# Weight loads of a second MoE issued by GpSimd instead of SyncE, and its raw tiles loaded a group earlier

## The chip, the cores and the metric

The kernel runs on one core of a Trainium2 chip. The metric is the device time of one execution in microseconds (us). TensorE (PE) multiplies matrices; VectorE (DVE), ScalarE (ACT) and GpSimd (POOL) work on tiles; SyncE (SP) and POOL issue the DMA transfers (loads and stores), which run on 16 DMA engines.

## The reference

Talking-heads attention, then two feed-forward blocks ("MoE" by name) on the 1792 tokens that come out of it:

```python
scores = scale * q @ k^T            # (4, 12, 448, 448)
attn = softmax(einsum(scores, w_pre)); attn = einsum(attn, w_post)
x = (attn @ v) as 1792 x 768
h = x @ w_in;  x = layernorm(h * softmax(h)) * g_ln @ w_out    # d_ff 1024
h = x @ w2_in; out = max(h, 0)**2 @ w2_out                     # d_ff 2048
```

All is float32; two of the four weight matrices come as float64 words, w2_in and w2_out among them, and the kernel makes float32 of them itself.

## The kernel before, in words

Every product is made of three float32r products: each operand is split into a rounded part (ACT's copy) and the rest (a subtraction on POOL or DVE). The kernel has three stages: the attention (to about 400 us), the first MoE (to about 655 us) and the second MoE (the rest). The change lies in the second MoE, apart from the place of some constants.

**The second MoE** goes over the tokens in two passes of 896, and in each over d_ff in 8 groups of 256 columns (`NE = 8`). `q` counts the groups of both passes, 0 to 15. In group q, PE makes the hidden products of the group (`prod`, line 1107: in the first pass four plain ones, "22", "21", "12", "11"; in the second pass seven, of sums and differences of the quadrants) and, in between, the output products of the group before, seven tiles y of 128 tokens (`y2`, line 1178; `ps_y` has two buffers). A list sets the order of a group's slots; in the first pass it is `SEQ_P = ["22", 4, "21", 5, 6, 3, "12", 0, 1, 2, "11"]`, where the numbers are y tiles. Tiles y of group 0 are copied out of PSUM by ACT (line 1187), those of the later groups are added by DVE (line 1189). ACT makes the squared relu of each hidden product (lines 1123 to 1125), DVE its rest (line 1120).

In each slot `k` further work is set by `plan(q)`: `split_ti` (line 1035 on ACT, line 1036 on POOL) makes `ti` from `ra`, the raw tile of w2_in; `split_to` (line 1043 on ACT, line 1044 on POOL) makes `to` from `ro`, the raw tile of w2_out. Each raw tile has one buffer, so the next load of it, `load_ra` (line 985) and `load_ro` (line 996), stands right behind the splits that read it:

```python
at(7, split_to, q, 0)
at(8, split_to, q, 1)
at(8, load_ro, n)
at(10, split_ti, n, "a11")
at(10, split_ti, n, "a12")
at(10, load_ra, n + 1)
```

**The stream.** `w2stream` makes float32 of the 96 pieces (128 x 256) of w2_in and w2_out; 60 of them during the first MoE, the rest in q = 0 to 5 of the second. A piece has a load of float64 words to `nraw` (four buffers; line 793, SP), a square on ACT (line 803) and a multiplication on POOL (line 804), which make a mask `nt`, three steps on DVE (lines 828, 832, 834) and a store to DRAM (line 811, SP), from where `ra` and `ro` are loaded later. `steps2(n)` advances the stream by n of its steps, three a piece.

**The second pass's tokens.** `mix_second` loads x2D tiles `xb` (line 917, SP), makes their differences on DVE (line 925) and stores these to `xtD` (line 931); it advances once a slot in q = 6. In q = 7 and 8 `load_xc` (line 966, SP) loads the operands `xr`, and `split_xc` splits them on ACT (line 977) and DVE (line 978) into `xc`. The buffers of `xb` are those in which the stream's `nt` lay.

Each engine works through its own instructions in the order in which the program names them, and a DMA issue that has to wait holds up everything behind it in its engine's queue.

Of the kernel before, what the change touches and what calls it, by code (L numbers as in the profile page):

```python
# [7 lines left out]
F32 = mybir.dt.float32  # L8
# [10 lines left out]
def kernel(  # L19
# [16 lines left out]
    nc = tc.nc  # L36
    B, D, _ = qT.shape
    H = w_pre.shape[0]
    S = v.shape[1]
    NT, DM = out.shape  # L40
    F1 = w1_in.shape[1]
# [7 lines left out]
    RH = R // 2  # L49
# [4 lines left out]

    ctx.enter_context(tc.manual_schedule())
    const = ctx.enter_context(tc.tile_pool(name="const", bufs=1, side="left"))
    mixc = tc.tile_pool(name="mixc", bufs=1, side="right")
    mixc_p = mixc.__enter__()
    dram = ctx.enter_context(tc.tile_pool(name="dram", bufs=1, space=bass.MemoryType.DRAM))
    xD = dram.tile([DM, NT], F32, name="xD")  # L60
    x2D = dram.tile([DM, NT], F32, name="x2D")
# [3 lines left out]
    w2oD = dram.tile([F2, DM], F32, name="w2oD")  # L65
    HT = NT // 4
    xtD = [dram.tile([4 * (DM // 2), HT], F32, name=f"xtD{i}") for i in range(2)]

    mask_sb = mixc_p.tile([128, 2, RH], F32, name="mask_sb")
    wp_raw = mixc_p.tile([128, H], F32, name="wp_raw")  # L70
    wq_raw = mixc_p.tile([128, H], F32, name="wq_raw")
    wpre_bd = mixc_p.tile([128, 64], F32, name="wpre_bd")
    wpost_bd = mixc_p.tile([128, H, RH], F32, name="wpost_bd")
    eps_sb = const.tile([128, 3], F32, name="eps_sb")
    g_sb = mixc_p.tile([128, F1 // 128], F32, name="g_sb")

    def narrow(raw, sq, t, eng=nc.vector):

# [390 lines left out]
    def run(part):  # L469
        for _ in part:  # L470
            pass
# [98 lines left out]
    for s in range(lo_s, NP + 2):  # L570
# [47 lines left out]
        for i in sorted(w1f):  # L618
            sq, t = w1f.pop(i)
# [43 lines left out]
    psa.__exit__(None, None, None)  # L663
    sspools[1].__exit__(None, None, None)
    late.__exit__(None, None, None)
    mixc.__exit__(None, None, None)


    K1 = F1 // 128
# [106 lines left out]
    NE = F2 // FE  # L776
# [76 lines left out]
    def steps2(n):  # L853
        for _ in range(n):
            next(stream, None)
# [77 lines left out]
    def mix_second():  # L933

        parts = [load_xb(1, 0), load_xb(1, 1)]
        yield True
        for c in range(HC):
            b11, b12, b21, b22 = qs = parts[c]
            for i in range(4):
                mix_x(qs, i, nc.vector)  # L940
                if i % 2:
                    yield True
            for name, b in zip(XT, (b11, b22, b12, b21)):
                store_xt(1, c, name, b)
            if c + 2 < HC:
                parts.append(load_xb(1, c + 2))
            yield True
# [3 lines left out]
    def load_xc(p, name):  # L951
        t0 = 2 * p * HT
        rs = []
        for c in range(HC):
            if ORDER.index(name) % 2:
                r = wi2a_p.tile([128, HT], F32, tag=("xb00", "xb01", "xb11")[c], name="xr", bufs=2)
            else:
                r = wi2a_p.tile([128, HT], F32, tag="xr", name="xr", bufs=3)
            if name in ("p1", "p2", "p3"):
                k, t = {"p1": (0, 0), "p2": (1, 0), "p3": (1, 1)}[name]  # L960
                r0 = (k * HC + c) * 128
                src = x2D[r0:r0 + 128, t0 + t * HT:t0 + (t + 1) * HT]
            else:
                r0 = (XT.index(name) * HC + c) * 128
                src = xtD[p][r0:r0 + 128]
            nc.sync.dma_start(out=r, in_=src)
            rs.append(r)
        xraw[p, name] = rs
# [11 lines left out]
    def load_ra(q):  # L980
        if q < NQ:
            f0 = (q % NE) * FE
            for k in range(2):
                t = wi2a_p.tile([128, HC, FE], F32, tag=f"ra{k}", name="ra", bufs=1)
                nc.sync.dma_start(
                    out=t,
                    in_=w2iD[k * HC * 128:(k + 1) * HC * 128, f0:f0 + FE].rearrange("(c p) f -> p c f", p=128),
                )
                ra[q, k] = t

    def load_ro(q):
        if q < NQ:
            for f in range(KE):
                t = m2_p.tile([128, DM], F32, tag=f"ro{f}", name="ro", bufs=1)
                r0 = (q % NE) * FE + f * 128
                nc.sync.dma_start(out=t, in_=w2oD[r0:r0 + 128, :])
                ro[q, f] = t

    def quad(q, f, k):
# [97 lines left out]
    def prod(q, name):  # L1097
        b = BANK[name]
        first = name not in ("p3", "p2", "p4")
        if first:  # L1100
            bank[b] = ps2_p.tile([128, 512], F32, tag=f"b{b}", name="ps_h2", bufs=1)
        pairs = PLAIN.get(name, ((name, name),))
        for j, (tn, xn) in enumerate(pairs):
            t = ti[q, tn]
            for c in range(HC):
                for i, (w, a) in enumerate(((0, 0), (0, 1), (1, 0))):
                    nc.tensor.matmul(  # L1107
                        out=bank[b][:, 0:HT],
                        lhsT=t[:, w, c],
                        rhs=xc[xn][:, a, c],  # L1110
                        start=(first and j == 0 and c == 0 and i == 0),
                        stop=(j == len(pairs) - 1 and c == HC - 1 and i == 2),
                        skip_group_check=not first,
                    )

    def lows():
        while low:
            r, f, t = low.pop(0)
            hi, lo = [gt[:, a, f, t * HT:(t + 1) * HT] for a in range(2)]
            nc.vector.tensor_tensor(out=lo, in0=r, in1=hi.bitcast(F32), op=ALU.subtract)  # L1120
# [75 lines left out]
    YO = [4, 5, 6, 3, 0, 1, 2]  # L1196
# [7 lines left out]
    def plan(q):  # L1204

        n = q + 1
        work = {}

        def at(k, f, *a):
            work.setdefault(k, []).append((f, a))  # L1210

        if q < SW:
            at(5, fin, q, "22")
            at(6, fin, q, "12")
            at(9, fin, q, "21")
            at(10, fin, q, "11")
# [3 lines that stand above are left out]
            if n < SW:  # L1220
                at(4, split_ti, n, "a21")
                at(4, split_ti, n, "a22")
                at(10, split_ti, n, "a11")
                at(10, split_ti, n, "a12")
            else:
                at(2, mix_w, n, 0)
                at(2, split_ti, n, "p1")
                at(3, mix_w, n, 1)
                at(3, split_ti, n, "p6")
                at(4, split_ti, n, "p5")  # L1230
                at(5, split_ti, n, "p7")
                at(10, split_ti, n, "p3")
                at(10, split_ti, n, "p2")
                at(10, split_ti, n, "p4")
            at(10, load_ra, n + 1)
        else:
            at(3, split_ti, n, "p1")
            at(3, mix_w, n, 0)
            at(4, mix_w, n, 1)
            at(5, split_ti, n, "p6")  # L1240
            at(6, split_ti, n, "p5")
            at(7, lambda q: square(hs.pop(q), 1, 1), q)
            at(7, split_ti, n, "p7")
            at(8, split_to, q, 0)
            at(10, split_ti, n, "p3")
            at(11, split_to, q, 1)
            at(11, load_ro, n)
            at(12, split_ti, n, "p2")
            at(13, split_ti, n, "p4")
            at(13, load_ra, n + 1)  # L1250
        return work

    load_ro(0)
    mx = mix_second()

# [8 lines left out]
    for q in range(NQ):  # L1264
        p = q // NE
        work = plan(q)
        if q == NE - 1:
            parts = [((1, name), c) for name in ORDER for c in range(HC)]
            load_xc(*parts[0][0])
            load_xc(*parts[HC][0])  # L1270
        seq = SEQ_P if q < SW else SEQ
        for k, x in enumerate(seq):
            if isinstance(x, str):
                prod(q, x)
                after(q, x)
            elif q:
                y2(q - 1, x)
            lows()
            for f, a in work.pop(k, []):
                f(*a)  # L1280
            if parts:
                t, c = parts[0]
                if q == NE - 1 and (t[1] in ("p2", "p4") or t[1] in ("p7", "p3") and k < 7):
                    t = None
                if t:
                    parts.pop(0)
                    split_xc(*t, c)
                    i = ORDER.index(t[1]) + 2
                    if c == HC - 1 and i < len(ORDER):
                        load_xc(1, ORDER[i])  # L1290
            if q <= NE - 3:
                if q or k > 5:
                    steps2(1 if x in YO[-3:] else 2)
            elif q == NE - 2:
                if k == 0:
                    run(stream)
                next(mx, None)
        assert not work
        if q < NE:
            assert len(narrowed) >= min(12 * (q + 2) + 6, len(w2pieces)), (q, len(narrowed))  # L1300
# [63 lines left out]
```

## Time and profile before

| | |
|---|---|
| time, median of 3 runs | 1124.88 us (1124.42 to 1127.59) |
| the profiled execution's own time | 1126.69 us |
| its span, first to last instruction | 1124.9 us |
| PE busy over the span | 1055.5 us (94%) |
| DVE, ACT, POOL busy | 680.0, 561.0, 629.8 us |
| mean granted clock of PE | 0.982 of full speed |

How to read it: the share of PE over the whole span hides that its gaps lie in places. Such places show in the windows (busy time of each engine in a stretch) and in the timeline (instructions in order of time, with the idle time before one and what ended it in square brackets).

### The profile page before, as it was taken

The numbers are of one execution on the slowest core, as the hardware profiler recorded it, in microseconds if no ns is written. First come the engines' busy times: TensorE is split into PE (matmuls) and PEld (weight loads), VectorE is DVE, ScalarE is ACT, GpSimd is POOL, SyncE is SP. The second block draws the span as 40 slices with busy tenths as digits, with TensorE's granted clock in tenths as the row PEclk, the third lists the DMA queues.
The fourth block names the chain that finished last, engine by engine and source line by source line (L and its number), as shares of the span: only waits on it lengthen the run. The fifth ranks groups of instructions, "written<-read, shape, count | busy, mean of one in ns | idle before, by whom it ended". The sixth has DMA issues, their size and how long they took to land.

```text
span 1124.9 us, 30957 instructions
## 1 busy us (share of the span) xinstructions
PE 1055.5 (94%) x12560; PEld 898.9 (80%) x12560; DVE 680.0 (60%) x1213; ACT 561.0 (50%) x1171; POOL 629.8 (56%) x808
## 2 busy tenths in 40 slices
PE   8789888988999899999999998999989999999998
PEld 3466555655666677989899998999988999999998
DVE  2556776766776625788887523677775752444444
ACT  3566566665777626533433444444324556444432
POOL 2656887877684736665564235545534565555520
PEclk8999999998999999999999999999999999999999
DMA  6686878778776634565654634444465441111102
GB/s 167 189 210 205 249 206 251 209 227 221 222 212 206 184 98 119 167 192 165 205 160 150 229 118 145 134 138 150 146 219 193 158 155 57 57 57 57 57 29 98
DMA packets 127182, 180.33 MB, mean 160 GB/s; under 512 B 24224, under 2 KB 99616, under 8 KB 127040
## 3 DMA queue, kind: packets, MB, share of 16 engines
q1 hardware_dynamic: 118196, 153.83, 45.1%
q0 software_dynamic: 6464, 22.60, 7.3%
q10 hardware_dynamic: 2380, 1.93, 0.6%
q8 instruction: 99, 1.62, 0.6%
q14 instruction: 43, 0.35, 0.1%
HBM read 101.63 MB, written 38.14 MB: 124 GB/s over the span
## 4 chain that ended last, share of the span: by engine, by line
PE 74%; DMA 8%; issue 7%; POOL 4%; ACT 3%; DVE 2%; SPq 1%; ACTq 0%; POOLq 0%; DVEq 0%
PE ps_y L1178 18%; PE ps_h L1107 14%; PE ps_o L764 9%; PE ps_h L459 9%; PE ps_ring L338 7%; PE ps_ring L299 7%; PE ps_pre L242 5%; PE ps_ring L208 4%; DMA sdst<-ssrc 4%; DMA ra<-w2iD 1%; ACT ssrc L215 1%; POOL ti L1036 1%; PE ps_tr L750 1%; POOL nt L804 1%; DMA v<-in_v_dram 1%
## 5 line engine op out<-in xcount | busy, mean ns | idle before, releaser
L1178 PE MATMUL ps_y<-to,gt 128*128 128x384 f32 x1332 | 244.6, 338 | 9.2 <-DVE y L1189 5.3
L1178 PEld LDWEIGHTS ps_y<-to,gt 128*128 128x128 f32 x1332 | 235.5, 190 | 12.5 <-ACT y L1187 3.9
L1107 PE MATMUL ps_h<-xc,ti 128*128 128x448 f32 x1080 | 227.3, 365 | 0.6 <-ACT h L1123 0.6
L1107 PEld LDWEIGHTS ps_h<-xc,ti 128*128 128x128 f32 x1080 | 201.9, 188 | 15.0 <-ACT h L1123 1.0
L299 PEld LDWEIGHTS ps_ring<-w,e 60*64 60x64 f32 (+1 forms) x5760 | 102.0, 137 | 66.5 <-issue 37.7
L318 DVE COPY at<-ps_ring 128x420 f32<-128x420 f32 x156 | 87.8, 610 | 111.3 <-PE ps_ring L299 111.2
L804 POOL TENSOR_SCALAR nt<-nt 128x256 f32<-128x256 f32 x96 | 111.5, 1161 | 64.3 <-ACT nt L803 55.2
L1189 DVE TENSOR_TENSOR y<-ps_y,y 128x768 f32<-128x768 f32 x97 | 92.3, 954 | 76.6 <-PE ps_y L1178 76.1
L299 PE MATMUL ps_ring<-w,e 60*64 60x60 f32 (+2 forms) x5760 | 110.2, 221 | 26.7 <-issue 17.5
L215 ACT COPY ssrc<-ps_ring 128x896 f32<-128x896 f32 x92 | 82.4, 907 | 102.8 <-PE ps_ring L208 80.8
L459 PE MATMUL ps_h<-w1i,xs 128*128 128x512 f32 x504 | 122.1, 400 | 0.6 <-POOL xs L704 0.6
L260 ACT ACTIVATE e<-ps_pre,nm 128x448 f32<-128x448 f32 x180 | 113.2, 639 | 15.4 <-DVE nm L253 13.5
L764 PE MATMUL ps_o<-zt,w1o 128*128 128x384 f32 (+1 forms) x720 | 120.4, 326 | 0.2 <-POOL w1o L690 0.2
L764 PEld LDWEIGHTS ps_o<-zt,w1o 128*128 128x128 f32 x720 | 117.0, 189 | 0.6 <-POOL w1o L690 0.6
L459 PEld LDWEIGHTS ps_h<-w1i,xs 128*128 128x128 f32 x504 | 95.1, 190 | 22.8 <-POOL xs L704 1.3
L253 DVE TENSOR_REDUCE nm<-ps_pre 128x1 f32<-128x448 f32 x180 | 103.3, 612 | 13.2 <-PE ps_pre L242 13.1
L338 PEld LDWEIGHTS ps_ring<-at,v 128*64 128x64 f32 x1536 | 80.7, 145 | 36.9 <-issue 12.9
L1036 POOL TENSOR_TENSOR ti<-ra,ti 128x384 fp32r<-128x384 f32 x56 | 59.5, 1075 | 89.9 <-ACT ti L1035 88.3
L208 PE MATMUL ps_ring<-k,q 64*64 64x448 f32 x752 | 100.6, 556 | 8.7 <-ACT ssrc L215 4.4
L1120 DVE TENSOR_TENSOR gt<-h,gt 128x448 fp32r<-128x448 f32 x64 | 48.9, 764 | 96.3 <-ACT gt L1125 91.6
L242 PE MATMUL ps_pre<-sdst,wpre_bd 64*64 64x448 f32 x720 | 99.5, 567 | 4.5 <-DMA sdst<-ssrc 2.5
L338 PE MATMUL ps_ring<-at,v 128*64 128x120 f32 (+1 forms) x1536 | 88.8, 274 | 14.3 <-issue 7.5
(105 smaller groups left out, 1388.3 us busy)
## 6 DMA issues: line engine op xcount, KB each, us to landing
sdst<-ssrc SPq DMA_DIRECT2D x166, 210.0 KB
nraw<-in_moe_w_in_dram SPq DMA_DIRECT2D x48, 256.0 KB
nraw<-in_moe_w_out_dram SPq DMA_DIRECT2D x48, 256.0 KB
ra<-w2iD SPq DMA_DIRECT2D x32, 384.0 KB
ro<-w2oD SPq DMA_DIRECT2D x32, 384.0 KB
w1raw<-in_moe_w_in_dram POOLq DMA_DIRECT2D x24, 256.0 KB, 6.4
w1raw<-in_moe_w_out_dram POOLq DMA_DIRECT2D x24, 256.0 KB, 5.9
w2iD<-nt SPq DMA_DIRECT2D x48, 128.0 KB
```

Source lines behind the costliest of these rows:

```text
L208: nc.tensor.matmul(out=ps[64 * u:64 * u + 64, e, 0:S], lhsT=qq[c][64 * e:64 * e + 64, p * n + u * half:p * n + u * half + 64], rhs=k[64 * ...
L215: (nc.vector.tensor_copy if dve else nc.scalar.copy)(ssrc[c][:, p:H:HP, :], ps[:, :, 0:S])
L242: nc.tensor.matmul(out=ps[b][64 * u:64 * u + 64, 0:S], lhsT=wpre_bd[64 * r:64 * r + m], rhs=ds[b][64 * r:64 * r + m], start=True, stop=True,)
L253: nc.vector.tensor_reduce(out=nm, in_=pres[s][b][:, 0:S], op=ALU.max, axis=AX.X, negate=True)
L260: nc.scalar.activation(out=e, in_=pres[s][b][:, 0:S], func=AF.Exp, bias=nms.pop((s, b)), scale=1.0, accum_out=sms[s][:, b:b + 1])
L299: nc.tensor.matmul(out=ps[64 * c:64 * c + 64, u, i0:i0 + ng * RH], lhsT=e[64 * u:64 * u + m, o:o + 64], rhs=w[64 * u:64 * u + m, b, g0:g0 ...
L338: nc.tensor.matmul(out=ps[64 * e:64 * e + 64, 0, q * 120:q * 120 + n], lhsT=t[:, g] if j < NJ else t[:, e, p], rhs=at[c][:, j * H + (g if ...
L459: nc.tensor.matmul(out=ps[:, u], lhsT=t[:, a, cc], rhs=w1i[cc][:, w, u * 512:(u + 1) * 512], start=(cc == 0 and a == 0 and w == 0), stop=( ...
L764: nc.tensor.matmul(out=ps[:, 0:width], lhsT=w1o[k][:, w, cc * 128:(cc + 1) * 128], rhs=zT[:, a, k, 0:width], start=(k == 0 and i == 0), st ...
L804: nc.gpsimd.tensor_scalar(out=t, in0=t, scalar1=2.0**-30, scalar2=2.0 - 2.0**-23, op0=ALU.is_ge, op1=ALU.mult)
L1107: nc.tensor.matmul(out=bank[b][:, 0:HT], lhsT=t[:, w, c], rhs=xc[xn][:, a, c], start=(first and j == 0 and c == 0 and i == 0), stop=(j == ...
L1178: nc.tensor.matmul(out=ps[:, u - u2[0], 0:DM // 2], lhsT=gt[:, a, f, o:o + 128], rhs=w[:, v, f, u * (DM // 2):(u + 1) * (DM // 2)], start= ...
```

## The change

Three edits. The constants of the attention (mask, w_pre, w_post, g_ln; 664 bytes a partition) move from a pool of their own on the right side of SBUF to the pool `const` on the left. The loads `ra` and `ro` are issued by GpSimd instead of SyncE. In the first pass of the second MoE the stream advances by two steps in every slot, where it advanced by one in the slots of y tiles 0, 1 and 2; and the first step of `mix_second`, which loads eight `xb` tiles, moves from the first slot of q = 6 to the end of the last slot of q = 5.

```diff
-    mixc = tc.tile_pool(name="mixc", bufs=1, side="right")
-    mixc_p = mixc.__enter__()
...
-    mask_sb = mixc_p.tile([128, 2, RH], F32, name="mask_sb")
+    mask_sb = const.tile([128, 2, RH], F32, name="mask_sb")
...
-    g_sb = mixc_p.tile([128, F1 // 128], F32, name="g_sb")
+    g_sb = const.tile([128, F1 // 128], F32, name="g_sb")
...
-    mixc.__exit__(None, None, None)
...
                 t = wi2a_p.tile([128, HC, FE], F32, tag=f"ra{k}", name="ra", bufs=1)
-                nc.sync.dma_start(
+                nc.gpsimd.dma_start(
...
-                nc.sync.dma_start(out=t, in_=w2oD[r0:r0 + 128, :])
+                nc.gpsimd.dma_start(out=t, in_=w2oD[r0:r0 + 128, :])
...
             if q <= NE - 3:
                 if q or k > 5:
-                    steps2(1 if x in YO[-3:] else 2)
-            elif q == NE - 2:
-                if k == 0:
+                    steps2(2)
+                if q == NE - 3 and k == len(seq) - 1:
                     run(stream)
+                    next(mx)
+            elif q == NE - 2 and k:
                 next(mx, None)
```

The order of instructions on three places. First SP at the start of the second MoE, where the loads of the stream begin; `x2D<-o` are the last stores of the first MoE. Before:

```order
L773 DMA x2D<-o_10064 128x256
L996 DMA ro<-w2oD 128x768 x2
L793 DMA nraw<-in_moe_w_in_dram 128x256 x3
L996 DMA ro<-w2oD 128x768 x2
L793 DMA nraw<-in_moe_w_in_dram 128x256
L985 DMA ra<-w2iD 128x3x256 x2
L793 DMA nraw<-in_moe_w_in_dram 128x256
L811 DMA w2iD<-nt 128x256
```

Now:

```order
L770 DMA x2D<-o_10060 128x256
L790 DMA nraw<-in_moe_w_in_dram 128x256 x5
L808 DMA w2iD<-nt 128x256
L790 DMA nraw<-in_moe_w_in_dram 128x256
L808 DMA w2iD<-nt 128x256
```

No ra or ro load stands between the raw loads of the stream any more. The second place is POOL in q = 0, from the splits of group 0's last `ti` on. Before:

```order
L804 TENSOR_SCALAR nt<-nt 128x256
L1044 TENSOR_TENSOR to<-ro,to 128x768
L804 TENSOR_SCALAR nt<-nt 128x256
L1044 TENSOR_TENSOR to<-ro,to 128x768
L804 TENSOR_SCALAR nt<-nt 128x256
L1036 TENSOR_TENSOR ti<-ra,ti 128x384 x2
L804 TENSOR_SCALAR nt<-nt 128x256 x3
```

Now:

```order
L801 TENSOR_SCALAR nt<-nt 128x256
L1041 TENSOR_TENSOR to<-ro,to 128x768
L801 TENSOR_SCALAR nt<-nt 128x256 x2
L1041 TENSOR_TENSOR to<-ro,to 128x768
L993 DMA ro<-w2oD 128x768 x2
L801 TENSOR_SCALAR nt<-nt 128x256
L1033 TENSOR_TENSOR ti<-ra,ti 128x384 x2
L982 DMA ra<-w2iD 128x3x256 x2
L801 TENSOR_SCALAR nt<-nt 128x256 x3
```

POOL has the four loads behind the splits that free their buffers, and one multiplication `nt` more ahead of the second `to`. The third place is SP from the end of the stream to q = 7. Before:

```order
L996 DMA ro<-w2oD 128x768 x2
L793 DMA nraw<-in_moe_w_out_dram 128x256
L985 DMA ra<-w2iD 128x3x256 x2
L811 DMA w2oD<-nt 128x256 x5
L917 DMA xb<-x2D 128x448 x8
L931 DMA xtD_72<-xb 128x448 x4
L917 DMA xb<-x2D 128x448 x4
L931 DMA xtD_72<-xb 128x448 x4
L996 DMA ro<-w2oD 128x768 x2
L931 DMA xtD_72<-xb 128x448 x4
L985 DMA ra<-w2iD 128x3x256 x2
L966 DMA xr<-x2D 128x448 x3
```

Now:

```order
L790 DMA nraw<-in_moe_w_out_dram 128x256
L808 DMA w2oD<-nt 128x256 x5
L914 DMA xb<-x2D 128x448 x8
L928 DMA xtD_69<-xb 128x448 x4
L914 DMA xb<-x2D 128x448 x4
L928 DMA xtD_69<-xb 128x448 x8
L963 DMA xr<-x2D 128x448 x3
```

Here too the ra and ro loads are gone from between the stream's stores, the xb tiles and the xr tiles; on SP alone the order of these is the same.

## Rows read from the trace of the kernel before

**Rows 1.** Windows of the two passes: start:end, length, then busy time.

```profile
640.00:887.00 247.00, 238.21 (x1291) 227.76 (x1290) 146.67 (x209) 105.88 (x209) 115.12 (x91) 0.99 0.47 151
887.00:1125.00 238.00, 233.43 (x1261) 225.86 (x1260) 110.07 (x143) 104.64 (x193) 112.18 (x96) 1.00 0.23 78
```

(The columns are PE, PEld, DVE, ACT and POOL, each with its count of instructions, then the granted clock of PE, the busy share of the DMA engines and GB/s.)

**Rows 2.** Timeline of PE in q = 1, and an ordinary y tile.

```profile
675.16 0.98 PE L1178 MATMUL ps_y<-to,gt 128*128 128x384 f32 x4 [0.28 <-POOL to L1044]
...
687.56 3.89 PE L1178 MATMUL ps_y<-to,gt 128*128 128x384 f32 x12 [3.61 <-ACT y L1187]
...
737.63 2.24 PE L1178 MATMUL ps_y<-to,gt 128*128 128x384 f32 x12
```

**Rows 3.** Timeline of PE in q = 6 and 7.

```profile
838.28 3.64 PE L1178 MATMUL ps_y<-to,gt 128*128 128x384 f32 x12 [3.11 <-DVE y L1189]
...
867.86 2.38 PE L1178 MATMUL ps_y<-to,gt 128*128 128x384 f32 x12 [0.95 <-DVE y L1189]
871.09 2.34 PE L1178 MATMUL ps_y<-to,gt 128*128 128x384 f32 x12 [0.85 <-DVE y L1189]
```

**Rows 4.** Windows around two gaps: PE busy, granted clock, DMA share, GB/s.

```profile
687.56:691.45 3.89, 3.89 (x13) 0.57 0.43 108
...
835.20:838.28 3.08, 0.00 (x1) 0.91 0.97 326
838.28:841.90 3.62, 3.62 (x13) 0.61 0.78 256
```

**Rows 5.** Timeline of ACT in q = 1.

```profile
685.37 0.43 ACT L803 ACTIVATE nt<-nraw 128x256 f32<-128x256 f32 x1 [5.56 <-DMA nraw<-in_moe_w_in_dram]
...
688.10 0.93 ACT L1035 CAST ti<-ra 128x384 fp32r<-128x384 f32 x2
...
691.49 0.80 ACT L1187 COPY y<-ps_y 128x768 f32<-128x768 f32 x1 [2.11 <-PE ps_y L1178]
...
695.13 0.55 ACT L1123 ACTIVATE h<-ps_h 128x448 f32<-128x448 f32 x1 [0.85 <-PE ps_h L1107]
...
697.22 0.80 ACT L1187 COPY y<-ps_y 128x768 f32<-128x768 f32 x1 [0.33 <-PE ps_y L1178]
```

**Rows 6.** Timeline of SP's queue at the end of q = 0.

```profile
677.89 1.53 SPq L985 DMA_DIRECT2D ra<-w2iD  x2
679.51 0.43 SPq L793 DMA_DIRECT2D nraw<-in_moe_w_in_dram  x1
```

**Rows 7.** Timeline of POOL at the end of q = 0.

```profile
671.80 1.13 POOL L804 TENSOR_SCALAR nt<-nt 128x256 f32<-128x256 f32 x1
673.01 2.10 POOL L1044 TENSOR_TENSOR to<-ro,to 128x768 fp32r<-128x768 f32 x1
...
676.61 2.41 POOL L1036 TENSOR_TENSOR ti<-ra,ti 128x384 fp32r<-128x384 f32 x2
```

**Rows 8.** Timeline of DVE in q = 0, 6 and 7.

```profile
670.04 1.96 DVE L832 SCALAR_TENSOR_TENSOR nt<-nraw,nt 128x256 uint32<-128x256 uint32 x1
...
672.66 0.41 DVE L834 SCALAR_TENSOR_TENSOR nt<-nraw,nt 128x256 uint32<-128x256 uint32 x1
...
833.83 0.63 DVE L925 TENSOR_TENSOR xb<-xb 128x448 f32<-128x448 f32 x1 [3.53 <-DMA xb<-x2D]
...
866.06 0.88 DVE L978 TENSOR_TENSOR xc<-xr,xc 128x448 fp32r<-128x448 f32 x1 [8.16 <-ACT xc L977]
```

**Rows 9.** Timeline of SP's queue in q = 6 and 7.

```profile
829.83 3.77 SPq L917 DMA_DIRECT2D xb<-x2D  x8
...
858.80 1.34 SPq L985 DMA_DIRECT2D ra<-w2iD  x2
860.19 1.43 SPq L966 DMA_DIRECT2D xr<-x2D  x3
```

**Rows 10.** Loads of v that POOL issues in the attention, line 186.

```profile
L186 POOL DMA_DIRECT2D v<-in_v_dram x12: 629/629/667, 38.6 to 330.1; - x12
...
DMA to landing us min/median/max: 4.9/6.7/9.8
```

(Duration of the issue in ns, least, median and most; then the time from issue to landing.)

More of the change, by code (lines that the diff above doesn't have):

```diff
@@ L67 @@
     xtD = [dram.tile([4 * (DM // 2), HT], F32, name=f"xtD{i}") for i in range(2)]
-    mask_sb = mixc_p.tile([128, 2, RH], F32, name="mask_sb")
[L70 to L73, printed above, removed]
+    mask_sb = const.tile([128, 2, RH], F32, name="mask_sb")
+    wp_raw = const.tile([128, H], F32, name="wp_raw")
+    wq_raw = const.tile([128, H], F32, name="wq_raw")
+    wpre_bd = const.tile([128, 64], F32, name="wpre_bd")
+    wpost_bd = const.tile([128, H, RH], F32, name="wpost_bd")
     eps_sb = const.tile([128, 3], F32, name="eps_sb")
-    g_sb = mixc_p.tile([128, F1 // 128], F32, name="g_sb")
+    g_sb = const.tile([128, F1 // 128], F32, name="g_sb")
     def narrow(raw, sq, t, eng=nc.vector):
```

## The prediction

> **What bounds the kernel now.** I read the windows first, to see where TensorE is not busy. From 640 to 887 us, which is the first pass of the second MoE, PE is busy 238.21 of 247.00 us; from 887 to the end 233.43 of 238.00 [rows 1]. So in this part PE sets the pace, POOL is busy under half of the time, and all that a better order of loads can give back is the 8.8 us of PE's gaps in the first pass, with what a gap costs behind it. The timeline of PE then names the gaps.
>
> In group q = 1 PE stops for 3.61 us at 684 us, released by ACT's copy of a y tile; at the start of the group it had stopped for 0.28 us [rows 2]. Around q = 6 and q = 7 it stops for 3.11, 0.95 and 0.85 us, each time released by DVE's add of a y tile [rows 3]. A gap costs more than its length: the 12 matmuls of a y tile take 2.24 us in the ordinary case [rows 2], but 3.89 and 3.64 us behind the two long gaps [rows 2, 3], where the granted clock fell to 0.57 and 0.61 of full speed [rows 4], that is mostly to the lower of its levels. Behind the two short ones they take 2.38 and 2.34 us [rows 3].
>
> So the gaps cost: at q = 1, 3.61 + (3.89 - 2.24) = 5.26 us; at q = 6, 3.11 + (3.64 - 2.24) = 4.51 us; at q = 7, 0.95 + 0.85 + 0.14 + 0.10 = 2.04 us. **Sum 11.8 us.**
>
> **What is late in each gap.** At q = 1 ACT sat 5.56 us before the square at 685.37, waiting for the load of a raw tile, with the y copies that PE waits for behind it in ACT's queue [rows 5]. That raw tile was issued by SP at 679.51 only, behind the two ra loads at 677.89 [rows 6], and the second of those waits for POOL's subtractions, which end at 676.61 + 2.41 = 679.02 [rows 7]. The raw tile's buffer had been free since DVE's last step on it, 672.66 + 0.41 = 673.07 [rows 8]. SP was blocked by a load whose turn had come too early.
>
> At q = 6 DVE waits 3.53 us for an xb tile before its first subtraction at 833.83, with the y adds behind it [rows 8]; SP issued the eight xb loads from 829.83 on [rows 9], at the tail of the rest of the stream. At q = 7 the first xc subtraction runs at 866.06 only, behind ACT's cast of a tile that SP loaded at 860.19, again right behind two ra loads at 858.80 [rows 8, 9].
>
> **The change, part by part.**
>
> *Constants.* 664 bytes a partition move from the first pool on the right to the first on the left. No instruction comes or goes, and nothing in this trace waits for them after the start. Price 0, and both bounds as well.
>
> *Loads by GpSimd.* SP loses its 64 ra and ro issues, each of which may wait for POOL. POOL's own subtraction is what they waited for, so on POOL they come at once. With SP free, the load for ACT at 685.37 is issued when its buffer is free, some 0.4 us after 673.07, which is 6 us earlier; even with the same 5.9 us from issue to use (679.51 to 685.37) it is there at 679.4, before y5's matmuls end. The gap of q = 1 goes. At q = 7 the loads no longer stand behind ra either, whose place in the queue held them until 858.80; the x tiles then go out behind the last xtD stores. That gap goes too.
>
> POOL pays for each issue. The nearest row is the v load, of the same 384 KB and issued by POOL in the attention: 0.629 us, and 6.7 us in the median to landing (4.9 to 9.8) [rows 10]. ra is in three pieces a partition where v is in one; so I take 0.63 us and keep 1.9 us (three times) as the upper end. Per group that is 4 x 0.63 = 2.5 us on an engine that was idle (247.00 - 115.12) / 8 = 16 us a group in the first pass and (238.00 - 112.18) / 8 = 16 us in the second [rows 1]. Off the path, therefore, but for one place, below. In the second pass ra lands later than by SP, by up to the 4 us between the first ra's old turn and POOL's last subtraction plus the longer landing; what it feeds is used by PE a whole group later, so I price that at 0; if the 16 us of cover were gone, it is rival C.
>
> *A faster stream and earlier xb loads.* `steps2` now runs two steps in every slot, where three of the eleven slots of a group had one (in q = 0 too). The stream is finished in the seventh slot of q = 5, and the eight xb loads, which wait for nt's stores, go out in the last slots of q = 5 instead of inside q = 6. The 4.51 us go. The steps' extra DVE work (one piece a group, three instructions of about 0.4 us each [rows 8]) falls among the adds of tiles 0, 1 and 2, after which PE has two products to do before the next y tile needs a bank.
>
> *What is late next.* At the start of q = 1 PE waits for POOL's low part of `to` [rows 2, 7]. In the new order one more nt multiplication stands ahead of it on POOL: 1.13 us [rows 7]. `to` ends at about 676.3 instead of 675.1, so the gap of 0.28 us becomes 1.4: **+1.2 us** (bounds 0.8 and 2.8: with or without a clock loss such as the long gaps had, 1.6).
>
> After that POOL issues two ro loads (1.26), one nt (1.13) and the two ti subtractions (2.41) before ra: with the small gaps between them the second ra goes out at about 681.9 and lands 6.7 us later, at 688.6. ACT must cast it (two casts, 0.93 us) before it copies y3. From the casts at 688.10 to the end of y0's copy at 698.02 ACT had 9.92 us, of which it idled 2.11 + 0.85 + 0.33 [rows 5]; so 6.6 us of work. PE will be there earlier than before by the gap and its clock loss less the new wait, 5.26 - 1.2 = 4.1 us, and y0's copy, which did no harm at 698.02, must then end by 693.9, or by 695.3 if it may use the time of one more tile (2.24 us less the copy's 0.80). Hence ra may land at 687.3 to 688.7 without harm. I price **+0.6 us**, the middle (0 at the later bound; at 9.8 us to landing 3 to 4; with 1.9 us an issue up to 2.5 us more).
>
> On the issue's price the v loads of this trace stay at 0.629 us while DVE works beside them [rows 10]. A rule of the Trainium skill speaks against that, SBUF — State Buffer, SBUF: two separate sides: a DMA issued by GpSimd can't write its descriptors while VectorE holds the port that the two share, and one of 620 ns became one of 3100 ns. By an estimate from that page POOL would lose 2.5 us an issue, 10 us a group, which would still fit under its idle time; but the four issues ahead of ra's landing at q = 1 would come 10 us later, and the sum would be near 0 instead of -10 (in rival C).
>
> **Sum.** -11.8 + 1.2 + 0.6 = **-10.0 us**. The profiled execution took 1126.69 us around a span of 1124.9, which is 1.8 us above the median of the runs shown, 1124.88 (1124.42 to 1127.59); its PE gaps are of the program, so I subtract from the median: **1114.9 us**. Three tenths of a per cent, 3.4 us, is what a measurement of this kernel can tell from no change.
>
> **Rivals.**
>
> A. *ACT waits again in q = 1.* The faster stream and POOL's later ra make ACT wait for a load before the y copies, and most of the first gap returns. For it: ACT's queue there keeps the same order of kinds, and the stream asks for each raw tile earlier than before. Against: the raw loads themselves start 6 us earlier. Landing at 9.8 us gives 3 us, plus 1.65 of clock: 1114.9 - 0.6 + 4.65 = 1119 us; with 1.9 us an issue up to 1121.
>
> B. *The transfers, not their turn, are the limit.* In the gap at 835 the DMA engines are 0.97 busy and move 326 GB/s [rows 4]. If the bytes merely queue elsewhere, the gaps of q = 6 and 7 stay (6.55 us): 1114.9 + 6.55 = 1121.5 us; if that of q = 1 stays too, 1126 us. Against: the xb loads were late in their start, not slow; from their first issue at 829.83 to DVE's use of it at 833.83 [rows 8, 9] are 4.0 us. The Trainium skill has a rule for this case, DMA: Bandwidth & Descriptors, Issuing engines are not separate DMA queues: issuing from several engines saves only the sequencer's issue time, since all run on the same DMA engines. The rows show something else to be saved, an issue's wait behind another's [rows 6]; no run here shows yet which weighs more.
>
> C. *POOL becomes the bound: slower than before.* If an issue on POOL blocks it far longer than 0.63 us, the gain goes first and POOL's 16 us of idle time a group after it. Each us more an issue brings ra at q = 1 4 us later (four issues), and ACT passes that on; at 3 us an issue 4 x 2.4 = 9.6 us of the gain are gone: 1124.5 us. From 16 / 4 = 4 us an issue the kernel slows. At 5 us it is 4 us a group over 15 groups, less the 10 us saved: about 1175 us; at 4.3 us about 1133. For it: DVE and POOL do hold each other up here, a DVE step of 0.41 us took 1.96 us at 670.04 [rows 8], when POOL split the first half of `to`. Against: the issues of v, with DVE at work beside them, took 0.629 us and 0.667 at most [rows 10]. This is the port rule of the page on SBUF named above, taken further than its figure goes.
>
> **How the numbers follow.** The forecast (all three gaps go, 1113 to 1117) has 0.58; A 0.24; B 0.12; C 0.06. Faster by over 0.3% (under 1121.5): the forecast, A, and a part of B, 0.85; within 0.3%: the rest of B, some of C's mild end, 0.10; slower 0.05. The range: below, all 11.8 us with no new wait and 1.5 us for what I have not seen, 1111.5; above, to A's end, 1121.
>
> **What would show it.** Right: no PE gap above 1 us between 680 and 880, the squares no longer waiting 5 us for raw loads, xb loads issued before q = 6, clock near 1.00 in every stretch. The step on `to`: a PE gap of about 1.4 us at 675, released by POOL. Wrong: a y copy of ACT released by a DMA or by ra in q = 1 (A); DVE waiting for xb or xr (B); issues on POOL above 2 us, PE gaps in the second pass released by POOL (C).

## The result, and the profile after

The changed kernel took 1116.99 us in the median of 19 runs (1105.17 to 1130.22), the kernel before, timed beside it, 1127.59 us (1123.44 to 1136.41, 19 runs). The ratio is 0.988, with a 95% interval of 0.9852 to 0.9907: faster by 10.6 us by the medians. The ratio is that of the means without the three slowest runs of the changed kernel, which lie over 1.5% above its fastest; with all 19 runs of each it is 0.989. The profiled execution took 1120.56 us, its span is 1118.8 us, the mean granted clock 0.986.

Runs of one kernel scatter by 1 to 2%, and in the profiles that scatter arises in the attention: two executions of the changed kernel (the one here and e11 below), 3.5 us apart in span, are 3.8 us apart where the attention ends and 0.1 us in the second MoE. What the change does to the second MoE is therefore read from rows here, not from times.

The two windows of the passes, in the kernel after (columns as in [rows 1]):

```profile
640.00:887.00 247.00, 244.83 (x1335) 232.94 (x1334) 153.75 (x217) 111.95 (x220) 142.47 (x130) 1.00 0.49 159
887.00:1119.00 232.00, 227.84 (x1219) 218.26 (x1217) 102.79 (x135) 99.42 (x182) 124.66 (x119) 1.00 0.21 72
```

PE's idle time in the first pass falls from 8.8 to 2.2 us, and the clock is at 1.00 in both windows. POOL's busy time rises from 115.12 to 142.47 us; its issues of loads are counted in it. The timeline of PE in q = 1, q = 6 and q = 7 after answers to [rows 2, 3]:

```profile
676.77 0.98 PE L1175 MATMUL ps_y<-to,gt 128*128 128x384 f32 x4 [1.53 <-POOL to L1041]
...
681.30 6.41 PE L1175 MATMUL ps_y<-to,gt 128*128 128x384 f32 x36
687.54 3.88 PE L1104 MATMUL ps_h<-xc,ti 128*128 128x448 f32 x18
691.26 6.41 PE L1175 MATMUL ps_y<-to,gt 128*128 128x384 f32 x36
...
838.46 6.41 PE L1175 MATMUL ps_y<-to,gt 128*128 128x384 f32 x36
...
867.89 6.42 PE L1175 MATMUL ps_y<-to,gt 128*128 128x384 f32 x36
```

A row of 36 is three y tiles without a break. The gaps of 3.61, 3.11, 0.95 and 0.85 us are gone, with the slow matmuls behind them; the wait for POOL's part of `to` has grown from 0.28 to 1.53 us. ACT in q = 1, against [rows 5]:

```profile
675.75 0.43 ACT L800 ACTIVATE nt<-nraw 128x256 f32<-128x256 f32 x1 [0.66 <-DMA nraw<-in_moe_w_in_dram]
...
682.40 0.43 ACT L800 ACTIVATE nt<-nraw 128x256 f32<-128x256 f32 x1 [3.48 <-DMA nraw<-in_moe_w_out_dram]
...
687.47 0.52 ACT L1032 CAST ti<-ra 128x384 fp32r<-128x384 f32 x1 [0.60 <-DMA ra<-w2iD]
```

The square still waits for a load once, for 3.48 us, but ACT has nothing queued there that PE lacks. The second ra is on hand for its cast at 687.47 after 0.60 us of waiting. POOL in the same place, and the durations of its issues (ns, least, median, most; for ra also the time from issue to landing):

```profile
672.05 2.52 POOL L801 TENSOR_SCALAR nt<-nt 128x256 f32<-128x256 f32 x2
674.65 2.06 POOL L1041 TENSOR_TENSOR to<-ro,to 128x768 fp32r<-128x768 f32 x1
676.66 1.14 POOL L993 DMA_DIRECT2D ro<-w2oD  x2
...
681.38 1.59 POOL L982 DMA_DIRECT2D ra<-w2iD  x2
```

```profile
L982 POOL DMA_DIRECT2D ra<-w2iD x32: 766/774/872, 621.3 to 1050.1; - x32
...
DMA to landing us min/median/max: 3.5/4.7/7.8
...
L993 POOL DMA_DIRECT2D ro<-w2oD x32: 539/562/622, 655.6 to 1071.0; - x32
```

Two pieces `nt` now stand ahead of `to` where one stood in [rows 7]. The xb loads of q = 6 start some 21 us earlier than in [rows 9], as SP's queue after shows:

```profile
808.51 3.94 SPq L914 DMA_DIRECT2D xb<-x2D  x8
```

**What was not foreseen.** With all that, the span of this execution is only 6.1 us shorter. The groups of PE's two kinds of matmul show why, first in the kernel before, then after (busy us, mean ns, idle time ahead):

```profile
L1178 PE MATMUL ps_y<-to,gt 128*128 128x384 f32 x1332 | 244.6, 338 | 9.2 <-DVE y L1189 5.3 <-ACT y L1187 3.6 <-POOL to L1044 0.3
L1107 PE MATMUL ps_h<-xc,ti 128*128 128x448 f32 x1080 | 227.3, 365 | 0.6 <-ACT h L1123 0.6
```

```profile
L1175 PE MATMUL ps_y<-to,gt 128*128 128x384 f32 x1332 | 241.3, 335 | 2.0 <-POOL to L1041 1.5 <-DVE y L1186 0.5
L1104 PE MATMUL ps_h<-xc,ti 128*128 128x448 f32 x1080 | 231.6, 368 | 0.6 <-ACT h L1120 0.6
```

The output products took 3.3 us less, which is the clock that the gaps had cost. The hidden products took 4.3 us more at the same granted clock. In the second pass, where PE has no gap, 36 of them in a row take 7.41 us instead of 7.25, in every group alike, as the chain of work that ended last shows for one late group of each kernel (start, us, count), before first:

```profile
1048.00 7.25 PE ps_h L1107 x36
```

```profile
1068.83 7.41 PE ps_h L1104 x36
```

That is 4.4 ns a matmul. (The timeline lets neighbouring groups overlap and has 7.42 and 7.58 us for such 36; the difference is the same. In the first pass it has 3.81 and 3.88 us for 18.) No instruction of these products has changed. What has changed is where their tiles lie. The built programs place the tiles as follows (first byte in a partition, of the first tile where there are several):

| | before | after |
|---|---|---|
| `ti`, weights of the hidden products | 37024 | 37760 |
| `xc`, the four moving tiles of the left pool | 70048 | 70784 |
| `xc`, the three of the right pool | 195296 | 195296 |
| `gt` and `to`, operands of the output products | 123360, 149216 | 123360, 149216 |

The constants' move pushes everything on the left 736 bytes on (664 bytes, each of the six tiles taking a multiple of 32). On the right, where their own pool stood to the end of the attention, it moves the attention's tiles by as much; the second MoE's tiles there lie as before. The operands of the output products, whose pace did not change, stayed.

### The profile page after: what moved, and what is told of

Read it like the earlier page. It is cut to its first block, busy times and chain, and to the rows that moved or that the text cites. A ratio compares the mean times of both kernels' runs of the same rounds, so it can differ in the third digit from the quotient of the medians.

```text
span 1118.8 us, 30912 instructions
## 1 busy us (share of the span) xinstructions
PE 1051.0 (94%) x12560; PEld 891.7 (80%) x12560; DVE 679.1 (61%) x1213; ACT 561.2 (50%) x1171; POOL 673.9 (60%) x872
## 3 DMA queue, kind: packets, MB, share of 16 engines
q8 instruction: 99, 1.62, 0.6%
## 4 chain that ended last, share of the span: by engine, by line
PE 70%; DMA 7%; issue 7%; POOL 5%; DVE 4%; ACT 4%; SPq 1%; ACTq 0%; POOLq 0%; DVEq 0%
PE ps_y L1175 18%; PE ps_h L1104 16%; PE ps_h L457 7%; PE ps_ring L297 7%; PE ps_o L761 6%; PE ps_ring L336 6%; PE ps_pre L240 5%; PE ps_ring L206 5%; DMA sdst<-ssrc 4%; ACT ssrc L213 2%; ACT e L258 1%; DMA w2oD<-nt 1%; POOL ti L1033 1%; DMA ra<-w2iD 1%; DVE nt L829 1%
## 5 line engine op out<-in xcount | busy, mean ns | idle before, releaser
L1175 PE MATMUL ps_y<-to,gt 128*128 128x384 f32 x1332 | 241.3, 335 | 2.0 <-POOL to L1041 1.5
L1175 PEld LDWEIGHTS ps_y<-to,gt 128*128 128x128 f32 x1332 | 233.0, 188 | 4.8 <-POOL to L1041 1.9
L1104 PE MATMUL ps_h<-xc,ti 128*128 128x448 f32 x1080 | 231.6, 368 | 0.6 <-ACT h L1120 0.6
L336 PEld LDWEIGHTS ps_ring<-at,v 128*64 128x64 f32 x1536 | 75.1, 138 | 33.3 <-issue 11.5
L800 ACT ACTIVATE nt<-nraw 128x256 f32<-128x256 f32 x96 | 40.5, 432 | 117.6 <-DMA w2oD<-nt 35.9
```

What stands on the lines that cost most here:

```text
L336: nc.tensor.matmul(out=ps[64 * e:64 * e + 64, 0, q * 120:q * 120 + n], lhsT=t[:, g] if j < NJ else t[:, e, p], rhs=at[c][:, j * H + (g if ...
L1104: nc.tensor.matmul(out=bank[b][:, 0:HT], lhsT=t[:, w, c], rhs=xc[xn][:, a, c], start=(first and j == 0 and c == 0 and i == 0), stop=(j == ...
L1175: nc.tensor.matmul(out=ps[:, u - u2[0], 0:DM // 2], lhsT=gt[:, a, f, o:o + 128], rhs=w[:, v, f, u * (DM // 2):(u + 1) * (DM // 2)], start= ...
```

## The experiments

**Theory H1:** the constants' move slows the hidden products by the new places of `ti` and `xc`. **Rival H2:** the loads issued by POOL slow them. And, for the gaps, what each of the two other edits does by itself.

To take the attention's scatter out, the table gives for each kernel the span, the start of the four matmuls that wait for `to` at the start of q = 1, their wait, and the rest: span less (start less wait). The last two columns are the time of all 1080 hidden products and that of 36 in a row in the second pass.

| kernel | span | start | wait | rest | 1080 | 36 |
|---|---|---|---|---|---|---|
| before | 1124.9 | 675.16 | 0.28 | 450.0 | 227.3 | 7.25 |
| changed | 1118.8 | 676.77 | 1.53 | 443.6 | 231.6 | 7.41 |
| e1 constants alone | 1123.6 | 667.14 | 0.17 | 456.6 | 233.0 | 7.41 |
| e2 all but the constants | 1120.6 | 682.72 | 1.62 | 439.5 | 227.3 | 7.25 |
| e3 32 bytes of padding | 1113.7 | 675.64 | 1.64 | 439.7 | 227.3 | 7.25 |
| e4 `ti` 32, left `xc` 64 bytes on | 1111.6 | 670.33 | 1.51 | 442.8 | 230.0 | 7.31 |
| e5 left `xc` 32 bytes on | 1112.4 | 670.74 | 1.52 | 443.2 | 230.1 | 7.38 |
| e6 loads alone | 1122.6 | 677.31 | 0.28 | 445.6 | 228.2 | 7.25 |
| e7 stream alone | 1120.4 | 675.26 | 1.63 | 446.8 | 227.3 | 7.25 |
| e8 64 bytes of padding | 1105.2 | 665.29 | 1.52 | 441.4 | 229.1 | 7.36 |
| e9 padding and turn | 1113.0 | 675.02 | 0.28 | 438.3 | 227.3 | 7.25 |
| e10 as e3 | 1109.1 | 671.17 | 1.64 | 439.6 | 227.3 | 7.25 |
| e11 changed again | 1115.3 | 673.12 | 1.54 | 443.7 | 231.6 | 7.41 |
| e12 96 bytes of padding | 1104.6 | 662.20 | 1.67 | 444.1 | 231.4 | 7.43 |

**e1, the constants' move alone** (the kernel before with this, and the same for the other five tiles of constants):

```diff
-    mask_sb = mixc_p.tile([128, 2, RH], F32, name="mask_sb")
+    mask_sb = const.tile([128, 2, RH], F32, name="mask_sb")
```

> The kernel before with the constants' move alone; the loads and the order of the steps stay. Theory H1: the move shifts all tiles of the left pools by 736 bytes (the weight tiles ti from byte 37024 to 37760 of the partition, the tiles xc of the pool wi2 from 70048 to 70784), and PE reads them more slowly there: a pair of 18 hidden products takes 3.88 us instead of 3.81, 36 in the second pass 7.4 instead of 7.25, the group of 1080 hidden products a mean near 369 ns instead of 365, 16 groups +4.4 us. The gaps of before (about 12 us from the start of the second MoE) stay, so this kernel is 0.4% slower than before: ratio 1.001 to 1.007. Rival H2, the loads issued by GpSimd slow the products: 3.81 us and 365 ns here, ratio 1.000. The prediction on record, which priced the move at nothing: ratio 1.000.

Measured: 36 hidden products in 7.41 us, and the gaps of before still there, as the timeline of PE shows:

```profile
679.53 4.21 PE L1178 MATMUL ps_y<-to,gt 128*128 128x384 f32 x12 [3.53 <-ACT y L1187]
833.41 4.18 PE L1178 MATMUL ps_y<-to,gt 128*128 128x384 f32 x12 [3.81 <-DVE y L1189]
```

H1 holds for the pace, H2 does not: no load was issued by POOL in the second MoE here. The rest is 6.6 us longer than before, 4.3 by pace and most of the remainder by a lower clock behind the gaps: 4.21 and 4.18 us for the 12 matmuls at a granted clock of 0.50 (3.89 and 3.64 us at 0.57 and 0.61 in [rows 2, 3, 4]), 245.8 us for all output products where before had 244.6, 233.0 for all hidden ones where the changed kernel has 231.6. But the time, 1127.35 us against 1128.9, is a ratio of 0.9981 (0.994 to 1.0023), not the 1.001 to 1.007 expected. Something ahead of the second MoE had become shorter; this is taken up below.

**e2, the other two edits without the constants' move** (shown in part; the rest as in the change).

```diff
-                nc.sync.dma_start(
+                nc.gpsimd.dma_start(
...
-                    steps2(1 if x in YO[-3:] else 2)
+                    steps2(2)
...
```

> Both other edits, the loads on GpSimd and the stream one group ahead, with the constants left in their own pool on the right. H1: hidden products as before (18 in 3.81 us, mean 365 ns), and the gaps of q=1, q=6 and q=7 gone as in the changed kernel (about 1.5 us left ahead of to): second MoE shorter by 9 to 10 us than before, 4 us shorter than the changed kernel; ratio 0.990 to 0.993 if the rest is like before. H2: 18 in 3.88 us and a mean of 368 ns, second MoE 6 us shorter than before, as in the changed kernel.

Measured: 7.25 us, 227.3 us for all, and the gaps gone; the rest is 10.5 us shorter than before and 4.1 shorter than the changed kernel's. The time, 1122.09 us, is a ratio of 0.9931 (0.9896 to 0.9965), the upper end of what was expected. The group of the output products in this kernel:

```profile
L1178 PE MATMUL ps_y<-to,gt 128*128 128x384 f32 x1332 | 241.0, 335 | 2.3 <-POOL to L1044 1.6 <-DVE y L1189 0.7
```

**e3, the changed kernel with 32 bytes of padding**, and **e10, the same timed once more**:

```diff
     g_sb = const.tile([128, F1 // 128], F32, name="g_sb")
+    pad0 = const.tile([128, 8], F32, name="pad0")
```

> The changed kernel with 32 bytes of padding behind the constants, so that the tiles of the second MoE's left pools start 32 bytes further on (ti at 37792, xc of wi2 at 70816); nothing else moves. H1 in its narrow form (what counts is where a tile starts within 64 bytes: the changed kernel's ti and xc start at a multiple of 64, before's 32 bytes past one): 18 hidden products back to 3.81 us, mean 365 ns or just under, second MoE 4 us shorter than the changed kernel. H1 in a wide form (the distance to some other tile, a larger step than 64 bytes): 3.88 us stays, or another figure. H2: 3.88 us, mean 368 ns.

> The changed kernel with 32 bytes of padding behind the constants once more, timed beside the changed kernel itself. If the pace of the hidden products is all that the padding changes: 227.3 us for the 1080 hidden products against 231.6, 0.4% under the changed kernel in time, as far as the scatter of the first part lets it be seen; ratio to before 0.983 to 0.988. If the places of the tiles were no cause: equal times and 231.6 us.

Measured, both times: 227.3 us and 7.25 us, the rest 439.7 and 439.6 us, 4 us under the changed kernel. 32 bytes give back what 736 had taken. The ratios to before are 0.9859 (0.9801 to 0.9917) and 0.9848 (0.9791 to 0.9905); e11 stood beside the second with 0.987, so in the time the 4 us are not to be told from the scatter.

**e4, padding ahead of `ti`**, and **e5, of the left `xc` alone**: 32 bytes at the start of the pool wi2a and 32 more at that of wi2, which puts `ti` at 37792 and `xc` at 70848; then at that of wi2 alone, `ti` at 37760, `xc` at 70816.

```diff
     wi2a_p = wi2a.__enter__()
+    pad1 = wi2a_p.tile([128, 8], F32, tag="pad1", name="pad1", bufs=1)
...
     wi2_p = wi2.__enter__()
+    pad2 = wi2_p.tile([128, 8], F32, tag="pad2", name="pad2", bufs=1)
```

> The changed kernel with 32 bytes of padding at the start of the pool wi2a and 32 more at the start of wi2: ti, ra and xb start 32 bytes past a multiple of 64, the tiles xc of wi2 still at a multiple of 64. If the place of the weights ti sets the pace: 18 hidden products in 3.81 us, mean 365 ns. If the place of the moving tiles xc does: 3.88 us, mean 368 ns (only the products with the four xc of wi2, not those with the three of the right pool, could be slow then; the trace of the changed kernel shows all alike, which speaks against it). H2: 3.88 us.

> The changed kernel with 32 bytes of padding at the start of the pool wi2 alone: ti stays at a multiple of 64 bytes (37760), the four tiles xc of wi2 start 32 bytes past one (70816). This is the complement of the padding of ti alone, which gave 7.31 us for 36 hidden products of the second pass, between before's 7.25 and the changed kernel's 7.41, and a mean of 367 ns. If the two operands' shares add up: 7.35 us here, mean near 367 ns. If the weights ti alone set the pace and the rest is chance: 7.41 us, 368 ns. If xc alone: 7.25 us, 365 ns.

Measured: 7.31 and 7.38 us, 230.0 and 230.1 us for all. Each padding gives back part of the 4.3 us (1.6 and 1.5), e3, which has `ti` as in e4 and `xc` as in e5, all of it. e4 is not `ti` alone: its `xc` lies 64 bytes further than in the changed kernel. The clean pairs are e5 and e3, which differ in the place of `ti` (7.38 and 7.25 us), and the changed kernel and e5, or e4 and e3, which differ in that of `xc` (7.41 and 7.38, 7.31 and 7.25). (With `ti` its pool's other tiles move, of which PE reads none.) The products "p5" of the second pass show the part of `ti` within each kernel, since their moving tile is one of the three in the right pool, which never move. Nine of them in the kernel before, the changed kernel, e4 and e5:

```profile
1029.89 1.96 PE L1107 MATMUL ps_h<-xc,ti 128*128 128x448 f32 x9
```

```profile
1023.00 2.01 PE L1104 MATMUL ps_h<-xc,ti 128*128 128x448 f32 x9
```

```profile
1016.14 1.96 PE L1106 MATMUL ps_h<-xc,ti 128*128 128x448 f32 x9
```

```profile
1016.77 2.01 PE L1105 MATMUL ps_h<-xc,ti 128*128 128x448 f32 x9
```

They are slow where `ti` lies as in the changed kernel, wherever the other `xc` lie.

**e8, 64 bytes of padding, and e12, 96 bytes** (`pad0` of 16 and 24 columns).

> The changed kernel with 64 bytes of padding behind the constants: ti starts at 37824, xc of wi2 at 70848, again multiples of 64 but not of 128 (the changed kernel's 37760 and 70784 are multiples of 128). If the place within 64 bytes counts: 36 hidden products in 7.41 us, mean 368 ns, as in the changed kernel, though the tiles have moved further than in the run with 32 bytes. If the place within 128 bytes counts, or any move away from the changed kernel's places: 7.25 us, 365 ns, or another figure.

> The changed kernel with 96 bytes of padding: ti at 37856, xc of wi2 at 70880, 32 bytes past a multiple of 64 as with 32 bytes of padding, but in another 64 bytes of each 128. If the place within 64 bytes is what makes 7.25 us of 36 hidden products: 7.25 us and 227.3 us for all. If a longer period counts, as the run with 64 bytes of padding hints (229.1 us where the changed kernel has 231.6): another figure, between 227.3 and 231.6 us.

Measured: 7.36 us with 64 bytes and 7.43 with 96, 229.1 and 231.4 us for all. So H1's narrow form falls: in e12 the tiles start 32 bytes past a multiple of 64, as in the kernel before, and are as slow as in the changed kernel. The places of `ti` and `xc` are the cause of the slower pace, e1 to e3 and e5 show that; the rule by which a place is fast or slow is open. Within a multiple of 128 bytes the kernels with the full pace have both at 32, but no place is slow by itself. In e8 both lie at 64, and the first pass's products, whose tiles are all in the left pools, run as in the kernel before; only the second pass is slower. Its products "p5", with `ti` at 64 and the moving tile of the right pool (at 96 in every kernel), take as long as in the slowest kernels, though the same right tile goes with 1.96 us when `ti` lies at 32. So the pair of places counts. The rows of e8, and 18 of the first pass in e12 for comparison:

```profile
753.68 3.81 PE L1105 MATMUL ps_h<-xc,ti 128*128 128x448 f32 x18
...
1037.16 2.02 PE L1105 MATMUL ps_h<-xc,ti 128*128 128x448 f32 x9
```

```profile
751.32 3.88 PE L1105 MATMUL ps_h<-xc,ti 128*128 128x448 f32 x18
```

**e6, the loads alone, and e7, the order of the stream alone**, each on the kernel before.

> The kernel before with the loads of the second MoE's weights on GpSimd, and nothing else. By the prediction's steps this alone frees SP: the gap of q=1 (3.6 us, ACT's y behind the square that waits for nraw) and those of q=7 (0.95 and 0.85 us) go, the gap of q=6 (3.1 us, the sums that wait for xb) stays, since the stream that issues those loads is not moved; left 3 to 5 us of PE's waits in the second MoE instead of 9.8. Rival: what frees q=1 is the order of the steps; then the 3.6 us stay.

> The kernel before with the order of the steps alone (two steps of the stream in each slot, the stream run out at the end of q=5, the sums of the second pass from q=6 on), the loads still on SP. By the prediction's steps the 3.1 us of q=6 go, the 3.6 us of q=1 stay or grow, since SP is still held by the loads' waits; left 4 to 7 us of 9.8. Rival: the gap of q=6 only moves to q=5, where the loads meet the same queue: 8 to 11 us left.

The timeline of PE in e6, with every gap over 0.3 us in q = 1 to 7:

```profile
836.19 4.18 PE L1178 MATMUL ps_y<-to,gt 128*128 128x384 f32 x12 [4.29 <-DVE y L1189]
```

and in e7:

```profile
675.26 0.97 PE L1178 MATMUL ps_y<-to,gt 128*128 128x384 f32 x4 [1.63 <-POOL to L1044]
686.55 3.81 PE L1178 MATMUL ps_y<-to,gt 128*128 128x384 f32 x12 [2.50 <-ACT y L1187]
835.08 2.34 PE L1178 MATMUL ps_y<-to,gt 128*128 128x384 f32 x12 [0.99 <-DVE y L1189]
863.26 2.36 PE L1178 MATMUL ps_y<-to,gt 128*128 128x384 f32 x12 [0.84 <-DVE y L1189]
866.64 2.34 PE L1178 MATMUL ps_y<-to,gt 128*128 128x384 f32 x12 [1.03 <-DVE y L1189]
```

The loads on POOL free SP, and with that the gaps of q = 1 and q = 7 go, while that of q = 6 stays (4.29 us, the xb loads issued at 827.53). The order of the stream takes most of q = 6 away and leaves the other two, with the longer wait for `to`. PE waits 6.0 us in e6 and 7.9 in e7 (9.8 before, 2.6 after), more than the 3 to 5 and 4 to 7 expected: in e6 the gap of q = 6 has grown from 3.11 to 4.29 us, in e7 0.99 us of it are left. Each edit removes the gaps that the prediction put down to it, the second all but this rest, and only both remove all.

**e9, padding and turn:** e3, and in q = 0 one step of the stream instead of two in the last three slots.

```diff
-                    steps2(2)
+                    steps2(1 if q == 0 and x in YO[-3:] else 2)
```

> The changed kernel with 32 bytes of padding behind the constants and, in q=0 alone, one step of the stream instead of two in the last three slots, as before the change, so that GpSimd comes to the second half of to one piece earlier. If the 1.53 us that PE waits for to in q=1 come from that one piece: 0.3 us left there as in the kernel before, second MoE some 1.2 us shorter than with the padding alone, 5.5 us shorter than the changed kernel; 36 hidden products 7.25 us; ratio to before 0.982 to 0.987, 0.4% under the changed kernel measured beside it. If the piece is only made up elsewhere: a wait of over 1 us at another place of q=1 to q=7, no gain over the padding alone.

**e11, the changed kernel again**, beside it:

> The changed kernel itself once more. If the slow pace belongs to the places of its tiles: 36 hidden products of the second pass 7.41 us and 231.6 us for all 1080, again, and 1.5 us ahead of to; ratio to before 0.986 to 0.991. If the pace varies from one execution to the next: another figure, down to 227.3 us.

Measured: in e9 the wait for `to` is back at 0.28 us and no other has come:

```profile
675.02 0.98 PE L1176 MATMUL ps_y<-to,gt 128*128 128x384 f32 x4 [0.28 <-POOL to L1042]
```

The rest is 438.3 us, 5.4 shorter than in e11 and 11.7 shorter than before. The time is 1111.02 us, a ratio of 0.982 (0.9774 to 0.9866), the lowest of all; the changed kernel beside it has 1116.95 us and 0.987 (0.9812 to 0.9927). These intervals overlap, so that e9 is the faster one rests on the rows. e11's rows repeat 231.6 us and 7.41 us to the digit: the pace belongs to the program, not to the execution.

## Why the prediction came out as it did

The forecast was 1114.9 us from 1124.88, less 10.0 us. By the medians timed together it is less 10.6, by the ratio's interval less 10.5 to 16.7. The gaps went as its steps said: e2, which has all of the sum and not the constants' move, is 10.5 us shorter in the second MoE. That the whole change came out near the same number is in part luck: two effects that come with the constants' move, neither of them in the sum, have opposite signs.

- **The gaps, -11.8 us.** PE's waits apart from that for `to` fell from 9.5 to 1.1 us, and the output products by 3.3 us: 8.4 + 3.3 = 11.7 us. e6 and e7 show that each gap had the cause named for it: SP held by loads that waited for POOL in q = 1 and 7, the late xb loads in q = 6.
- **The wait for `to`, +1.2 us.** 1.53 - 0.28 = 1.25 us, without a loss of clock. One piece more ahead of it on POOL is the cause: e9 takes that piece away, and the wait with it.
- **ra at q = 1, +0.6 us.** It measured 0: the second cast ran at 687.47, inside the 687.3 to 688.7 named as harmless. Two errors made that up: the second ra went out at about 682.2, a little later than forecast, and was there at most 5.3 us later, where the sum had 6.7 from the v loads. Rival A did not come: ACT's 3.48 us of waiting for a raw tile lie ahead of no y copy that PE needs.
- **An issue on POOL, 0.63 us.** Measured 0.56 us for ro and 0.77 for ra, 0.87 at most, with DVE busy 62% of the first pass. Rival C did not come. The Trainium skill, SBUF — State Buffer, SBUF: two separate sides, has a load of GpSimd take 3100 ns instead of 620 while VectorE holds the port that the two share; none of the 64 issues shows that, the longest took 0.87 us. Whether any step of VectorE held the port during one of them, no run here shows.
- **The transfers (rival B).** The xb loads move the same bytes and no longer delay PE. By the Trainium skill, DMA: Bandwidth & Descriptors, Issuing engines are not separate DMA queues, another issuing engine saves only issue time. e6 shows that more is saved here: SP's loads no longer wait behind one that is not yet allowed to start, and the gaps of q = 1 and q = 7, 3.61 and 1.80 us, go.
- **The constants, 0 us with both bounds 0: the step that failed.** "No instruction comes or goes, and nothing in this trace waits for them" was true, and not enough: the move places the tiles of two pools anew, and the hidden products took 4.3 us more.

The second MoE adds up: -11.7 + 1.25 + 4.3 = -6.2 us, where the table shows 443.6 - 450.0 = -6.4.

The rest of the gain lies ahead of the second MoE. The last group of attention matmuls starts at 404.4 to 411.2 us (mean 406.9) in the four profiles with the constants in their own pool, and at 392.2 to 404.9 (mean 399.5) in the ten with the constants moved: 7 us, read from single profiles with a standard deviation of 3 and 4 us. This agrees with e1, whose time does not rise although its second MoE is 6.6 us longer. Why is open. One row differs between these two sets of profiles without overlap: the time of the packets in the queue that holds SP's transfers, for the first 400 us (packets, MB, share of 16 engines), before first, then after:

```profile
q1 hardware_dynamic: 47917, 58.96, 51.8%
```

```profile
q1 hardware_dynamic: 47720, 58.84, 49.7%
```

That is 56.2 us of an engine for each MB (0.518 x 6400 / 58.96) against 54.1; over all profiles 56.2 to 57.0 with the constants in their own pool and 53.5 to 55.1 with them moved. The largest transfer of that queue goes from the tiles `ssrc` to the tiles `sdst` in rows of 1792 bytes, and their first bytes go from 84512 to 85248 and from 127520 to 128256, from 32 bytes past a multiple of 256 to a multiple of 256. The traces' records of single packets put the difference there: the 21552 packets of 1792 bytes in that queue, 20784 of them this transfer's, took 2116.7 us of an engine before and 1989.0 after, all its other packets 1109.6 and 1104.4. In the median such a packet takes 78 to 80 ns in the four profiles and 74 ns in each of the ten. The 127.7 us over 16 engines are 8.0 us, about what the attention gains; that the attention waits for this transfer no run shows.

The Trainium skill, DMA: Bandwidth & Descriptors, How a descriptor splits into AXI transactions, says that a piece which does not start at a multiple of 256 bytes begins with a fetch from the multiple below, whose unused bytes cost beats (of 32 bytes) too. An estimate from that page is 57 beats instead of 56 a row, 1.8%, where these packets' time differs by 6%. No kernel here moved these tiles alone, and others of the attention moved with them, so the cause of the shorter attention is argued, not shown.

## What to carry to other kernels

A load whose turn comes before its buffer is free blocks everything behind it in its queue; find it by following the waiting engine to the DMA, the DMA to its issue, and the issue to what stood ahead of it, and put such loads on the engine whose work frees the buffer. When tiles move within SBUF, look up which other tiles move with them, and compare the pace of unbroken runs of the same matmul before and after, at equal granted clock: a few ns a matmul over a thousand is worth as much as a gap. Try some tens of bytes of padding at the end of a pool, in more than one size, before giving the pace up: here 32 bytes gave the pace back, 64 in part, and 96 did not.

## What the runs showed of the hardware

- The same 36 matmuls of 128 x 448 took 7.25 us in some programs and 7.31 to 7.43 us in others with other first bytes of their weights and moving tiles, always at a granted clock of 1.00 and with the same instructions. Shifts of 32, 64 and 96 bytes from the changed kernel's places gave 7.25, 7.36 and 7.43 us. Both operands count, and as a pair: moving tiles at one place in the right pool went with 1.96 us for 9 matmuls or with 2.01 to 2.02, by the place of the weights.
- An issue of 384 KB by POOL took 0.56 us for tiles in one piece a partition (ro) and 0.77 us for tiles in three (ra).
- Packets of 1792 bytes, 96% of them between SBUF tiles, took 78 to 80 ns in the median in the four profiles with both tiles 32 bytes past a multiple of 256, and 74 ns in the ten with both at a multiple. That this is the cause is not shown.
